# An attention + GELU kernel on one core: planner reserve by unit size, three more GELU chunks on VectorE, and two load times moved

## The chip, the cores and the metric

The kernel runs on one core of a Trainium2 chip. The time is device microseconds for one execution; 5 runs are taken and the median is the number that counts. The engines are named as in the profile: PE (TensorE, matmuls), PEld (its weight loads), DVE (VectorE), ACT (ScalarE), POOL (GpSimd, which here only issues DMAs) and SP (SyncE, which here only issues DMAs).

## The reference

Attention over keys that are pooled 4 x 4, and then a feed-forward layer with a sigmoid-approximated GELU:

```python
# q (4, 12288, 128), kv (4, 384, 32, 128), w_sr (128, 128)
kv_pool = kv.reshape(B, H // r, r, W // r, r, C).mean(axis=(2, 4))   # r = 4: 768 keys per batch
k = v = kv_pool.reshape(B, -1, C) @ w_sr
s = (q @ k.transpose(0, 2, 1)) / sqrt(C)
a = softmax(s)
x = (a @ v).reshape(49152, 128)
h = x @ w_in                                  # w_in (128, 2048)
g = h * (1 / (1 + exp(-1.702 * h)))
out = g @ w_out                               # w_out (2048, 128), out (49152, 128) float32
```

## The kernel before

**Tiles.** The 49152 rows are cut into 96 groups of 512 rows. A chunk is one 128 x 512 tile of intermediate values. An attention group has 6 chunks (768 keys by 128), a feed-forward group has 16 (2048 features by 128). The work goes in two rounds of 48 groups: attention of round 1, feed-forward of round 1, attention of round 2, feed-forward of round 2.

**Units.** ACT takes a unit of up to three chunks in one instruction: PE fills up to three PSUM banks (0 to 2 or 3 to 5, in turn; L347 for attention, L593 for the feed-forward), and one ACTIVATE writes exp (L349) or GELU (L595) of the whole unit to SBUF (tile `ag`). The first two units have 1 chunk, the next 28 have 2, all others have 3, but for the last 8 of the kernel, which have 2 again. PE then drains the chunks: attention chunks in matmuls of 129 columns (L360; a step of `drain_attn` is three matmuls) and feed-forward chunks in matmuls of 512 columns (L603). The last group is drained by `drain_last` (L631), where the last 16 matmuls need the last ACT unit. DVE evicts the sums (L383 and L386 after attention, L614 after the feed-forward).

**VectorE's own share.** DVE computes some chunks without ACT. 24 attention chunks of groups 48 to 51 and 8 "rolling" chunks (the last key chunk of groups 38, 44, 57, 63, ...) go through a polynomial (L428 to L441). The "lent" chunks are feature chunk 15 of some feed-forward groups of round 2: PE fills one bank (L406), `lent_gelu` runs 15 DVE instructions on it (L450 to L472), and the result goes to a buffer `aside` of three slots, from where PE drains it (L603 out of `aside`). `early_fits` says when such a chunk may begin: a lent chunk of group i not before group i - 2 is being filled, a rolling chunk not before its queries are in SBUF. The drain of group i begins only when the lent chunk of i is made.

**Order.** The kernel writes the order of all engines by hand. A planner runs while the program is written: it keeps a model time `now` for PE, `end[p]` for ACT's end of unit p, `dve` for VectorE and `free` for the banks. One model step is one matmul of 512 columns. A unit takes ACT 0.295 + 1.978 steps per chunk; a `drain_attn` step is 0.78, a `drain_moe` step 1.0; half a reciprocal of `lent_gelu` is RECIPROCAL = 10.5. After filling unit n + 2 the planner puts drains and other jobs ahead of the fill of unit n + 3 as long as they end before `limit`:

```python
limit = end[-1] - K - HANDOVER if n + 3 < len(seq) else 1e9     # K = 3, HANDOVER = 1.0
```

`end[-1]` is ACT's end of unit n + 2, the last one filled, and K stands for the fill of unit n + 3. A fill of unit p starts no earlier than `end[p - 2] + HANDOVER / 2`, because it writes the banks that unit p - 2 leaves.

**Loads.** Queries come as bf16 in 24 blocks s of four groups. From block 3 on, POOL's queue casts a block in DRAM (`cast_q`, L209) and SP's queue loads it transposed (`load_qT`, L215, after a one-column DVE memset of the buffer, L214). `background(i)` issues these at the start of attention group i: `TURN` gives the transposing loads, `CAST` the casts. A `gate()` is a DVE memset (L517) followed by a POOL memset (L518), so that POOL's queue stays behind the order of DVE. The load of `w_in` (L548) stands at group 27 and that of `w_out` (L551) at 28. On SP the transposing loads share one queue with `put_away` (L500) and `bring_back` (L506), which transpose the attention output through DRAM.

Of the kernel before, what the change touches and what calls it, by code (L numbers as in the profile page):

```python
# [24 lines left out]
def kernel(  # L25
# [10 lines left out]
    FCH = d_ff // 128  # L36
# [5 lines left out]
    GB = NG // B  # L42
    SB = NS // B
    K = 3
# [53 lines left out]
    def acc_bf():  # L98
        return acc().bitcast(BF)
# [18 lines left out]
    kv_tiles, kv_sums, pooled, pTs, kTs, vs = {}, {}, {}, {}, {}, {}  # L118
# [86 lines left out]
    qTs = {}  # L205

    def cast_q(s):
        sl = slice(s * SG, (s + 1) * SG)
        nc.gpsimd.dma_start(out=q_bf[sl, :].rearrange("(p i) c -> p (i c)", p=128),  # L209
                            in_=q_flat[sl, :].rearrange("(p i) c -> p (i c)", p=128))  # L210

    def load_qT(s):
        qTs[s] = qpool.tile([128, 1, SG], BF, name="qT")
        nc.vector.memset(qTs[s][:, 0, 0:1], 0.0)  # L214
        nc.sync.dma_start_transpose(out=qTs[s], in_=q_bf[s * SG:(s + 1) * SG, :])  # L215


    QS = 3
    qs = [x_tile(XS - 1 - JC - s) for s in range(QS)]

    def load_q(s, lo, hi):
        nc.gpsimd.dma_start(  # L222
            out=qs[s].rearrange("p (g e) -> p g e", g=4)[:, lo:hi, :],
            in_=q_flat[s * SG + lo * G:s * SG + hi * G, :].rearrange("(g p i) c -> p g (i c)", p=128, i=4))

    def transpose_q(g):
        s = g // 4
        if g % 4 == 0:
            qTs[s] = qpool.tile([128, 1, SG], BF, name="qT")
        ps = acc_bf()[:, 0:G].rearrange("p (i t) -> p i t", i=4)  # L230
        for i in range(4):
            o = (g % 4) * G + i * 128
            nc.tensor.transpose(ps[:, i, :], qs[s][:, o:o + 128], ident)  # L233
        dst = qTs[s][:, 0, (g % 4) * G:(g % 4 + 1) * G].rearrange("p (t i) -> p t i", i=4)
        src = ps.rearrange("p i t -> p t i")
        if g == 0:
            nc.scalar.copy(dst, src)
        else:
            nc.vector.tensor_copy(dst, src)
# [86 lines left out]

    early = range(NG // R, NG // R + EARLY)
    rolling = [(i, JC - 1) for i in [*range(38, NG // R, 6), *range(57, 90, 6)]]
    lent = [(g, FCH - 1) for g in range(52, 94, 3)]
    aside = agpool.tile([128, K, 512], BF, name="aside")  # L330

    def weights(c):
# [112 lines left out]
    def lent_gelu(ps, out):  # L445
# [23 lines left out]
        for m in (0, 256):  # L469
            nc.vector.reciprocal(b[:, m:m + 256], a[:, m:m + 256])  # L470
            yield RECIPROCAL
        nc.vector.scalar_tensor_tensor(out, raw, -LN2 / 1.702, b, MUL, MUL)  # L472
# [4 lines left out]
    made, used = {}, []  # L477
# [4 lines left out]
    def early_fits(p, i, jc):  # L482
        if (i, jc) in rolling:
            group = seq[p][1][0][0] if seq[p][0] == "a" else seq[p][1][0][0] // (NG // R) * (NG // R) + NG // R - 1
            return (i // GB, jc) in vs and i // 4 - 1 <= group // 4 and len(used) > rolling.index((i, jc)) - K
        if (i, jc) in lent:
            return seq[p][0] == "m" and seq[p][1][0][0] >= i - 2 and len(used) > len(rolling) + lent.index((i, jc)) - K
        return low and min(slot_of.values()) >= low and (2, JC - 1) in vs
# [24 lines left out]
    def gate():  # L513

        one = gate_tile[:, gates[0] % 8:gates[0] % 8 + 1]
        gates[0] += 1
        nc.vector.memset(one, 0.0)  # L517
        nc.gpsimd.memset(one, 0.0)  # L518

    TURN = {6: 3, 7: 4, 8: 5, 20: 6, 21: 7, 22: 8, 30: 9, 32: 10, 35: 11, 40: 12}  # L520
    CAST = {0: [5], 13: [6], 14: [7], 15: [8], 25: [9, 10], 26: [11, 12]}
    CAST_MOE = {20: 13, 21: 14, 22: 15, 23: 16, 33: 17, 34: 18, 35: 19, 36: 20, 37: 21, 38: 22, 39: 23}

    def background(i):

        first_round = i < GB * 2
        s = TURN.get(i, NS) if first_round else i // 4 + 3 if i % 4 == 0 else NS
        if s < NS:
            load_qT(s)
        if i in CAST:  # L530
            gate()
            for s in CAST[i]:
                cast_q(s)
        if i in (10, 12):
            gate()
            for jc in range(i % 10 * 3 // 2, i % 10 * 3 // 2 + 3):
                load_chunk(1, jc)
        if 0 <= i - 16 < JC:
            extras.append((key_and_value, 1, i - 16))
        if 0 <= i - 15 < JC:  # L540
            extras.append((pool_chunk, 1, i - 15))
        if i in (28, 33, 38):
            put_away(0, (i - 28) // 5)
        if i in (31, 36, 41):
            bring_back(0, (i - 31) // 5)
        if i == 27:
            gate()
            nc.gpsimd.dma_start(out=w_in_sb, in_=moe_w_in)  # L548
        if i == 28:
            gate()  # L550
            nc.gpsimd.dma_start(out=w_out_sb, in_=moe_w_out.rearrange("(o p) c -> p o c", p=128))  # L551

# [99 lines left out]
    seq, todo = [], []  # L652
# [90 lines left out]
    FIXED, CHUNK, SWITCH, HANDOVER, EVACUATE = 0.295, 1.978, 6.0, 1.0, 4.5  # L743
# [2 lines left out]
            transpose_pooled: (0.9, 3.6), make_k: (0.8, 3.2), make_v: (0.8, 3.7)}  # L746
    COPY = {pool_chunk: 1.5, key_chunk: 1.5, value_chunk: 1.5, key_and_value: 2.8, transpose_q: 3.2}
    SMALL = 0.26
    RECIPROCAL = 10.5
    PAUSE = 4.0  # L750
    end, extra_at = [], 0.0
    source, dve = None, 0.0
# [41 lines left out]
    for n in range(len(seq)):  # L794
        fill(n + 2)
        jobs(n + 3)
        while True:
            room = room_ahead()
            limit = end[-1] - K - HANDOVER if n + 3 < len(seq) else 1e9
            bank = free[next_acc()]  # L800
            f = None
            if extras and now >= max(extra_at, bank):
                f, *args = extras[0]
            if steps and dve <= now + 2.0:
                early_step()
            near = todo and todo[0][0] == "m" and todo[0][2] > 10
            if not f and not near and not steps and early_todo and early_fits(min(n + 2, len(seq) - 1), *early_todo[0]) and dve <= now + 2.0 and now >= bank:
                f, args = early_fill, early_todo[0]
            if f and max(now, bank) + COST[f][0] > limit + (0.0 if f is early_fill else 4.5) and room >= 4 * K:
                f = None  # L810
            if f:
                now = max(now, bank) + COST[f][0]
                f(*args)
                free[last_acc] = dve + 1.0 if f is early_fill else copied(f)
                if f in (transpose_pooled, make_k, make_v):
                    on_dve(2.5)
                extra_at = max(now + PAUSE, dve + 1.5 if f in (transpose_pooled, make_k, make_v) else 0.0)
                if f is early_fill:
                    pass
                else:  # L820
                    extras.pop(0)
                continue
            if not source:

                if todo_early and not any(early_waits(t) for t in range(todo_early[0][1], todo_early[0][1] + TS)):
                    source = todo_early
                else:
                    source = todo
            if not source:
                break  # L830
            kind, i, c = source[0]
            needs = at[("at" if kind == "a" else kind, i, c)]
            cost = K * SMALL if kind == "a" else 1.0
            halved = kind == "a" and i // TS < SPLIT
            first_of = (c == 0 or halved) and (kind == "m" or i % TS == 0)
            if source is not todo_early and (needs > n or (kind == "a" and first_of and at["at", i + TS - 1, c if halved else 1] > n)
                                             or (kind == "m" and first_of and (i, FCH - 1) in lent
                                                 and made.get((i, FCH - 1), 1e9) > now + 1.0)
                                             or (kind == "a" and (early_waits(i) or first_of and early_waits(i + TS - 1)))):
                if first_of:  # L840
                    source = None
                break
            start = now if source is todo_early else max(now, end[needs] + HANDOVER)
            if first_of:
                start = max(start, bank)
            if start + cost > limit and not (room < 2 * K + 1 or (room < 4 * K and start == now)):
                if first_of:
                    source = None
                break
            now = start + cost  # L850
            (drain_attn if kind == "a" else drain_moe)(i, c)
            source.pop(0)
            if kind == "a" and i // 4 in early:
                early_left -= 1
                if not early_left:
                    low = 0
            if (halved or c == (1 if kind == "a" else FCH - 1)) and (kind == "m" or i % TS == TS - 1):
                source = None
# [31 lines left out]
```

The softmax here doesn't subtract the row's maximum and nothing guards it: scores larger than these inputs give would overflow.

## Time and profile before

| what | value |
|---|---|
| median of 5 runs | 950.36 us (950.16 to 951.31) |
| the profiled execution's own time | 950.16 us |
| its span in the profile | 948.4 us |
| PE busy | 935.0 us (99%) |
| ACT busy | 934.9 us (99%) |
| DVE busy | 536.3 us (57%) |
| POOL busy | 66.5 us (7%) |
| mean granted TensorE clock | 1.00 |

The page gives busy time by engine, by slices of time and by groups of instructions. The end of a matmul in it is modelled, and some matmul records are missing, so how full PE is must be read from the starts of matmuls and from the count of weight loads (one for each matmul), not from PE's busy share. The time outside of the span is 1.8 us.

### The profile page before, as it was taken

How to read it: one execution, taken by the hardware profiler on the slowest of the kernel's cores; microseconds unless marked ns; L12 is line 12 of the kernel's file. 1: busy time of each engine (PE TensorE's matmuls, PEld its weight loads, DVE VectorE, ACT ScalarE, POOL GpSimd, SP SyncE). 2: the span in 40 equal slices, each digit the busy share in tenths (PEclk: the TensorE clock that was granted, in tenths of full speed). 3: DMA queues.
4: the chain of work that ended last, by engine and by line, in shares of the span. 5: the costliest groups of instructions: out<-in, count | busy, mean ns of one | idle time of the engine just before them, and what ended most of it. 6: DMA issues, size and time to landing. Idle time of an engine off the chain costs nothing.

```text
span 948.4 us, 15310 instructions
## 1 busy us (share of the span) xinstructions
PE 935.0 (99%) x6201; PEld 503.0 (53%) x6314; DVE 536.3 (57%) x1035; ACT 934.9 (99%) x710; POOL 66.5 (7%) x114
## 2 busy tenths in 40 slices
PE   8999999999999999999999999999999999999998
PEld 4677776444444444454446777754444444444444
DVE  5643653102577777778655765365666665566631
ACT  6999999999999999999999999999999999999998
POOL 3101001420000232000000000000000000000000
PEclk9999999999999999999999999999999999999999
DMA  9999932999868799764335683562222222222222
GB/s 210 208 170 198 203 62 45 159 125 174 158 130 120 111 153 117 123 103 79 64 56 116 130 164 74 132 122 36 43 36 44 34 46 34 45 33 45 34 45 45
DMA packets 372855, 95.46 MB, mean 101 GB/s; under 512 B 346720, under 2 KB 370400, under 8 KB 372320
## 3 DMA queue, kind: packets, MB, share of 16 engines
q1 hardware_dynamic: 344000, 62.36, 37.4%
q0 software_dynamic: 28512, 31.99, 22.2%
q8 instruction: 49, 0.80, 0.4%
q14 instruction: 22, 0.18, 0.1%
q10 hardware_dynamic: 272, 0.13, 0.0%
HBM read 52.49 MB, written 48.76 MB: 107 GB/s over the span
## 4 chain that ended last, share of the span: by engine, by line
ACT 88%; PE 9%; DMA 2%; issue 1%; DVE 0%; POOL 0%; POOLq 0%
ACT ag L595 71%; ACT ag L349 17%; PE banks L347 4%; PE banks L360 3%; DMA qT<-q_bf 1%; DMA x<-in_kv_dram 1%; PE banks L139 0%; PE banks L593 0%; PE banks L631 0%; ACT L595 0%; PE banks L233 0%; PE banks L603 0%; ACT L349 0%; DVE kT L163 0%; POOL x L222 0%
## 5 line engine op out<-in xcount | busy, mean ns | idle before, releaser
L595 ACT ACTIVATE ag<-banks 128x1536 bf16<-128x1536 f32 (+1 forms) x510 | 682.2, 1508 | 0.0
L593 PE MATMUL banks<-x,w_in_sb 128*128 128x512 bf16 x1485 | 407.5, 379 | 2.0 <-ACT ag L595 0.3
L603 PE MATMUL banks<-ag,w_out_sb 128*128 128x512 bf16 x1476 | 403.2, 379 | 2.0
L349 ACT ACTIVATE ag<-banks 128x1536 bf16<-128x1536 f32 (+2 forms) x192 | 245.8, 1442 | 3.6 <-PE banks L233 2.3
L603 PEld LDWEIGHTS <-w_out_sb 128*128 128x128 bf16 x1520 | 148.5, 98 | 178.0 <-issue 0.9
L593 PEld LDWEIGHTS <-w_in_sb 128*128 128x128 bf16 x1522 | 147.3, 98 | 170.4 <-issue 1.1
L614 DVE STREAM_TRANSPOSE o_sb<-banks 128x512 f32<-128x512 f32 x95 | 67.9, 715 | 210.9 <-PE banks L603 195.2
L360 PEld LDWEIGHTS <-ag 128*128 128x128 bf16 x2272 | 146.1, 98 | 46.3 <-issue 0.6
L360 PE MATMUL banks<-v,ag 128*128 128x129 bf16 x2272 | 163.7, 220 | 0.2
L347 PE MATMUL banks<-qT,kT 128*128 128x512 bf16 x499 | 145.0, 379 | 3.5 <-DVE kT L163 1.0
L439 DVE SCALAR_TENSOR_TENSOR ea<-ea,eb 128x512 f32<-128x512 f32 x128 | 87.9, 686 | 3.2
L383 DVE RECIPROCAL rec<-banks 128x3 f32<-128x3 f32 x124 | 22.3, 180 | 95.9 <-PE banks L360 95.9
L386 DVE TENSOR_TENSOR x<-banks,rec 128x384 bf16<-128x384 f32 x124 | 69.2, 558 | 4.3
L347 PEld LDWEIGHTS <-kT 128*128 128x128 bf16 x544 | 46.3, 98 | 26.5 <-DVE kT L163 1.7
L470 DVE RECIPROCAL eb<-ea 128x256 f32<-128x256 f32 x28 | 47.6, 1726 | 0.5
L173 POOL DMA_DIRECT2D kvs<-in_kv_dram x32 | 40.5, 1318 | 16.0 <-DMA kvs<-in_kv_dram 12.5
L428 DVE TENSOR_SCALAR ea<-banks 128x512 f32<-128x512 f32 x32 | 22.1, 692 | 32.9 <-PE banks L412 32.6
L463 DVE SCALAR_TENSOR_TENSOR ea<-ea,eb 128x512 f32<-128x512 f32 x56 | 38.3, 684 | 1.6
L518 POOL MEMSET gate_tile<- 1x1 f32 x37 | 3.9, 105 | 328.2 <-DVE gate_tile L517 328.2
L434 DVE SCALAR_TENSOR_TENSOR eb<-eb,ea 128x512 f32<-128x512 f32 x32 | 22.1, 690 | 0.9
L450 DVE TENSOR_SCALAR qT<-banks 128x512 f32<-128x512 f32 x14 | 9.7, 692 | 17.2 <-PE banks L406 16.9
L441 DVE SCALAR_TENSOR_TENSOR ag<-ea,ee 128x512 bf16<-128x512 f32 x24 | 16.5, 688 | 0.7
(83 smaller groups left out, 266.4 us busy)
## 6 DMA issues: line engine op xcount, KB each, us to landing
out_dram<-o_sb SPq DMA_DIRECT2D x380, 64.0 KB, 2.0
kvs<-in_kv_dram POOLq DMA_DIRECT2D x32, 384.0 KB, 6.3
q_bf<-in_q_dram POOLq DMA_DIRECT2D x21, 512.0 KB, 6.8
x_bf<-x SPq DMA_DIRECT2D x13, 768.0 KB, 5.8
x<-in_kv_dram POOLq DMA_DIRECT2D x11, 512.0 KB, 10.1
x_bf<-x SPq DMA_DIRECT2D x6, 384.0 KB, 4.6
x<-in_q_dram POOLq DMA_DIRECT2D x5, 256.0 KB, 15.4
x<-in_kv_dram SPq DMA_DIRECT2D x1, 1024.0 KB, 5.0
```

What stands on the lines that cost most here:

```text
L173: nc.gpsimd.dma_start(out=kv_sums[b][:, i2], in_=kv_p[b, i, w, :, i2], **({"accum_op": ADD} if n else {}))
L347: nc.tensor.matmul(ps[:, k, :], kTs[i // GB][:, jc * 128:(jc + 1) * 128], rhs, start=True, stop=True)
L349: nc.scalar.activation(place([("a",) + c for c in chunks]), ps, AF.Exp, scale=scale)
L360: nc.tensor.matmul(av_of[u][:, k * (C + 1):(k + 1) * (C + 1)], weights(("a", i, jc))[:, o:o + T], vs[i // GB][:, jc, 0:C + 1], start=(jc = ...
L386: nc.vector.tensor_tensor(to, ps[:, :, 0:C], rec.unsqueeze(2).broadcast_to([128, TS, C]), MUL)
L439: nc.vector.scalar_tensor_tensor(a, a, COEFFS[k], b, ADD, MUL)
L463: nc.vector.scalar_tensor_tensor(a, a, COEFFS[k], b, ADD, MUL)
L470: nc.vector.reciprocal(b[:, m:m + 256], a[:, m:m + 256])
L593: nc.tensor.matmul(ps[:, k, :], w_in_sb[:, fc * 128:(fc + 1) * 128], x[:, g % (4 * XS) * G:(g % (4 * XS) + 1) * G], start=True, stop=True)
L595: nc.scalar.activation(place([("m",) + c for c in chunks]), ps, AF.Gelu_apprx_sigmoid)
L603: nc.tensor.matmul(o_of[g], w_out_sb[:, fc, :], weights(("m", g, fc)), start=(fc == 0), stop=(fc == FCH - 1))
L614: nc.vector.transpose(o_sb, o_of.pop(g))
```

## The change

Six edits:

- `limit` keeps free the chunks of the unit that is filled next, `len(seq[n + 3][1])`, instead of 3 always. It differs only ahead of units with fewer than 3 chunks.
- 17 lent chunks instead of 14: groups 52, 54, 57, 59, ... 89, 92 (two and three groups apart in turn) instead of 52, 55, ... 91.
- RECIPROCAL in the planner is 8.2 instead of 10.5.
- The cast of query block 9 goes from group 25 to 16, with a gate of its own; the casts of 10 and 11 stand at 26, that of 12 at 27; the loads of `w_in` and `w_out` go from groups 27 and 28 to 28 and 29.
- The transposing load of block 9 goes from group 30 to 25.
- `early_fits` asks of a rolling chunk that its queries were turned by PE (noted in `turned`), or that their block was loaded, is at most one block ahead of the group being filled, and is none of the first three.

```diff
+    turned = set()
+
     def transpose_q(g):
         s = g // 4
+        turned.add(g)
...
-    lent = [(g, FCH - 1) for g in range(52, 94, 3)]
+    lent = [(g, FCH - 1) for g in range(52, 94) if g % 5 in (2, 4)]
...
-            return (i // GB, jc) in vs and i // 4 - 1 <= group // 4 and len(used) > rolling.index((i, jc)) - K
+            return (i // GB, jc) in vs and (i in turned or i // 4 in qTs and i // 4 - 1 <= group // 4 and i >= 4 * QS) and len(used) > rolling.index((i, jc)) - K
...
-    TURN = {6: 3, 7: 4, 8: 5, 20: 6, 21: 7, 22: 8, 30: 9, 32: 10, 35: 11, 40: 12}
-    CAST = {0: [5], 13: [6], 14: [7], 15: [8], 25: [9, 10], 26: [11, 12]}
+    TURN = {6: 3, 7: 4, 8: 5, 20: 6, 21: 7, 22: 8, 25: 9, 32: 10, 35: 11, 40: 12}
+    CAST = {0: [5], 13: [6], 14: [7], 15: [8], 16: [9], 26: [10, 11], 27: [12]}
...
-        if i == 27:
+        if i == 28:
             gate()
             nc.gpsimd.dma_start(out=w_in_sb, in_=moe_w_in)
-        if i == 28:
+        if i == 29:
             gate()
             nc.gpsimd.dma_start(out=w_out_sb, in_=moe_w_out.rearrange("(o p) c -> p o c", p=128))
...
-    RECIPROCAL = 10.5
+    RECIPROCAL = 8.2
...
-            limit = end[-1] - K - HANDOVER if n + 3 < len(seq) else 1e9
+            limit = end[-1] - len(seq[n + 3][1]) - HANDOVER if n + 3 < len(seq) else 1e9
```

## The prediction

> **What bounds the kernel now.** I read the page's busy shares first, then the windows view of the last stage, then the waits of PE, ACT and SP, and last the timeline around each wait.
>
> ```profile
> PE 935.0 (99%) x6201; PEld 503.0 (53%) x6314; DVE 536.3 (57%) x1035; ACT 934.9 (99%) x710; POOL 66.5 (7%) x114
> ...
> 700.00:800.00 100.00, 99.53 (x456) 45.36 (x464) 64.12 (x89) 100.00 (x75) 0.00 (x0) 1.00 0.25 38
> ```
>
> The second line is 100 us of feed-forward of round 2. ACT runs 75 units in 100.00 us, 1.333 us each, with no gap: it is full. The columns in the brackets count instructions: 464 weight loads, so 464 matmuls, of which 8 have no record. In the timeline three 512-column matmuls start every 0.647 us (917.63, 918.28, 918.92), 0.2157 each. 464 x 0.2157 = 100.1 us: PE is full as well.
>
> Here a rule of the Trainium skill speaks against that reading. "Perfetto Trace Analysis", section "Identifying the Most-Contended Engine", says that matmul busy time is a poor measure and that the busy share of the weight loads should be used. By it PE, at 45 to 53%, has half its time free, ACT alone sets the time, and what ACT is spared comes off the end. By the starts, PE has nothing free, and sparing ACT alone gives nothing beyond the places where PE waits for ACT. I go by the starts. So I look for gains on both engines and take the smaller.
>
> Where does PE still wait? After the start-up there are three places.
>
> ```profile
> 33.13 0.59 PE L347 MATMUL banks<-qT,kT 128*128 128x512 bf16 x2
> 33.56 0.50 PE L360 MATMUL banks<-v,ag 128*128 128x129 bf16 x6
> 34.04 0.59 PE L347 MATMUL banks<-qT,kT 128*128 128x512 bf16 x2
> 34.47 0.50 PE L360 MATMUL banks<-v,ag 128*128 128x129 bf16 x6
> ```
>
> First, the units of two chunks at the beginning. A cycle is 0.915 us (33.13 to 34.04, and so on to 37.71). Its work is 2 x 0.2157 + 6 x 0.0567 = 0.77 us (twelve 129-column matmuls take 0.68: 39.51 to 40.19). PE stands 0.146 us in each cycle, waiting for ACT to give the banks back.
>
> ```profile
> 92.26 4.53 SPq L215 DMA_TRANSPOSE qT<-q_bf  x1
> ...
> 99.91 0.39 PE L412 MATMUL banks<-qT,kT 128*128 128x512 bf16 x1 [0.25 <-DMA qT<-q_bf]
> ...
> 101.16 1.45 ACT L349 ACTIVATE ag<-banks 128x1536 bf16<-128x1536 f32 x1 [0.32 <-PE banks L347]
> ```
>
> Second, the transposing load of block 9, issued at group 30, lands 7.6 us later, when PE already stands at the rolling chunk of group 38 that needs it. From 99.16, six matmuls would end at 99.50; the next starts at 99.91, so PE loses 0.41 us. ACT stands too: by the starts of its units it loses 0.44 us there (0.32 of it seen as idle).
>
> ```profile
> 935.54 0.38 PE L603 MATMUL banks<-ag,w_out_sb 128*128 128x512 bf16 x1
> 936.24 0.59 PE L593 MATMUL banks<-x,w_in_sb 128*128 128x512 bf16 x2 [0.32 <-ACT ag L595]
> 936.67 0.59 PE L603 MATMUL banks<-ag,w_out_sb 128*128 128x512 bf16 x2
> 937.16 0.59 PE L593 MATMUL banks<-x,w_in_sb 128*128 128x512 bf16 x2
> ...
> 941.75 0.59 PE L593 MATMUL banks<-x,w_in_sb 128*128 128x512 bf16 x2
> 942.19 3.07 PE L631 MATMUL banks<-w_out_sb,ag 128*128 128x128 bf16 x52
> ```
>
> Third, the units of two chunks at the end: 0.27 us at 936.24 (one matmul there has no record), four times 0.056 (0.915 - 4 x 0.2157), 0.1 at 940.82: 0.6 us. Yet behind the last fill PE has a queue of 52 matmuls, 3 us, where ACT's last unit ends at 943.5 and only the last 16 matmuls need it; these start at about 944.2. So PE stood still while it had work that it did later, and the end lies 0.6 us behind what ACT would allow.
>
> **The change part by part.**
>
> *Three more lent chunks.* The feed-forward of round 2 has 751 chunks for ACT instead of 754: 245 units of three and 8 of two, where it was 246 and 8. ACT is spared one unit, 1.33 us. PE's matmuls stay the same, only their place changes: 0 for PE. DVE gets 15 instructions per chunk, by the rows of the page and of the groups view: 4 x 0.684 (L463) + 2 x 1.726 (L470) + 4.86 for the other nine = 11.05 us, 33 us for three. "ScalarE: Activation LUTs", "Rules for kernel authors", says of exp and gelu that ScalarE is the only option; by price it is right, as a chunk costs ACT 0.444 us and DVE 25 times that. If DVE were on the path, the edit would cost 33 us. The row that decides is
>
> ```profile
> L614 DVE STREAM_TRANSPOSE o_sb<-banks 128x512 f32<-128x512 f32 x95 | 67.9, 715 | 210.9 <-PE banks L603 195.2
> ```
>
> DVE waits 195 us for PE ahead of this eviction. Cost 0, under that cover; without it see the second rival. An eviction caught behind a DVE step has cost PE 0.107 us (641.69, 852.67), twice in 14 chunks: 0.02 us for three.
>
> *RECIPROCAL 8.2.* Half a reciprocal takes 1.726 us, 8.0 steps of 0.2157. The model now agrees; the DVE steps of a chunk are written 2 x 2.3 x 0.2157 = 1.0 us closer. No cost, and what makes two groups' distance possible.
>
> *The reserve.* Ahead of units of two chunks `limit` moves one step later. In steps from `end[p - 2]`: the fill starts at 0.5 and ends at 2.5; `limit` was 8.5 - 4 = 4.5, so two drains of 0.78 fit (4.06), not three (4.84); the next fill may start at 4.75. That is the standing time: 0.69 steps, 0.149 us by the model, 0.146 in the trace. Now `limit` is 5.5 and a third drain fits. Nine matmuls and a fill are 0.94 us, over the cycle's 0.915, so PE becomes full, and ACT loses nothing while the delay stays below the second unit's reserve. Six such cycles stand from 32.6 to 37.7 (0.89 us), four smaller waits for ACT between 27.6 and 32.2 add about 0.35: 1.2 us. The waits for a fresh kT at 19 to 25 (0.6 of the idle that the waits view gives) may be partly filled too; between 0 and 0.6 I take 0, since the first drains exist only from 18.7. A reordering there could also push a fill back; its bound below zero is another loss of the size that ACT's starts show there already, 0.6. At the end, feed-forward drains cost 1.0 and two used up 4.5 exactly; three fit now. All 0.6 us of standing can be filled from the queue.
>
> *Block 9.* The load moves from the memset at 92.1 to group 25, whose gate is at 77.85. Its cast, behind gate 16 at about 54 (gate 15 is at 51.9), follows the cast of block 8, which lands at 65.1, and lands near 68, casts being 2.5 apart at 89.7 and 92.1. So the load lands near 86 and the 0.41 us on PE and 0.44 on ACT go. The next thing late would be block 11 (lands 112.3, rolling chunk of 44 near 121): not late. *What is moved past:* on SP, `put_away` of group 28, issued at 73.7, now stands behind this load and goes at about 82; its readers `bring_back` lie at 96.8 and later, and the feed-forward starts at 142: 55 us of cover. The casts of 10 and 11 stay in place or come earlier; that of 12 comes 2 us later and is wanted at 120. `w_in` and `w_out` land at 94.6 and 98.3 now, about 2 us later then; wanted at 142. Blocks 6 to 8 share the DMA engines with the new cast: up to 2.5 us later, with 9 us between block 6's landing (69.2) and group 24 (about 78). POOL has nothing behind gate 16 until 77.9. One gate more is 0.06 us of DVE. *early_fits* changes nothing here: for groups 38 and 44 and later the block is in `qTs` whenever the old condition held. All of this 0.
>
> **Sum.** PE: 1.2 + 0.41 + 0.6 = 2.2 us. ACT: 1.33 + 0.44 = 1.77, plus the 0.6 by which the end lies behind ACT: 2.4. The smaller is 2.2. Against the profiled execution, 950.16 - 2.2 = 947.96; the median lies 0.2 above it, so 948.2.
>
> **The rivals.**
>
> *Given back on PE (36%).* The third drain finds nothing ready, or the new order makes other waits (a fill behind an accumulator bank, an eviction behind a DVE step, 0.1 to 0.3 us apiece, as at 54.76, 122.37 and 566.52). Then only the 0.41 of block 9 and part of the 0.6 stay: 0.4 to 1.4 us, 949.0 to 950.0, and ACT idles instead. For it: PE had such waits in every attention stage. Against: at 40 us 58 chunks had been filled and some 28 drained (114 matmuls of L360, four a chunk), so there is work to take. That the change does nothing at all is only possible for `early_fits`.
>
> *VectorE late at two groups' distance (14%), slower.* A lent chunk takes 13.6 us from L450 to the end of L472 (894.5 to 908.1), evictions included; two groups last 13.4 (L614 every 6.69). A second chunk that waits for the first makes the drain of its group wait, and PE stands with nothing to do. The margin now: the last chunk is made at 908.1, the drain of its group starts near 913.3. So it decides when DVE is over 5.2 us behind. Eight pairs are two apart; if each is 0.6 us beyond the margin, PE loses 4.8 us, 953. Against it: the three groups after each pair give 6.7 us back, and the chain shrinks by 1.0.
>
> *ACT alone decides (within the first case).* If the weight-load rule were right, 1.77 to 2.4 us: 948.0 to 948.6. The time hardly tells it from mine; PE's waits do.
>
> **How the numbers follow.** A measurement of this kernel can tell about 0.2%, 1.9 us. My forecast, 50%, lies at 947 to 948.5, the lower end with the kT waits and some of ACT's early losses won too. It is over the bound only just, so much of the 36% lies right beside it. The range 946.8 to 951.2 takes in the forecast, the first rival and a reordering that costs 0.8; outside are the slow rival and a few in a hundred on either side.
>
> **What would show it.** ACT has 509 GELU activations (L595) instead of 510, L470 runs 34 times. Fills near 33 to 37 are 0.94 apart with nine matmuls between some of them. The 0.25 wait of L412 is gone and the load lands near 86. Near the end three drains stand between fills, and fewer than 52 L631 follow the last fill. I am wrong if waits of PE for DVE grow beyond 1 us, if the first stage of ACT loses more than now, or if L603 out of `aside` waits for L472.

## The result, and the profile after

| what | before | after |
|---|---|---|
| median | 950.36 us (45 runs) | 949.27 us (25 runs) |
| ratio, 95% interval | | 0.9987 (0.9982 to 0.9992) |
| the profiled execution's own time | 950.16 us | 949.27 us |
| its span | 948.4 us | 947.2 us |

The change wins 1.1 us, 0.13%. The forecast was 2.2 us: the time lies inside the range (946.8 to 951.2), but so does the time of the kernel before, and the likeliest case, faster by more than 0.2%, did not come about. The span of the profile fell by more than the time: its median is 947.1 us over the executions of the changed kernel and 948.5 to 948.6 for the kernel before (taken beside the later runs). The time outside of the span rose from 1.8 us to 2.1 us, in every execution alike (2.07 to 2.18). What takes it is not in the profile. In the changed kernel the lines of the core loops stand three further down: L596 and L606 are the fill and the drain of the feed-forward, L350 and L363 those of attention, L415 and L409 the single fills for VectorE, L634 the drain of the last group.

First the page of the changed kernel (busy times, the chain that ended last, the reciprocals of the lent chunks), then one row of its windows view:

```profile
PE 934.5 (99%) x6200; PEld 502.8 (53%) x6314; DVE 568.8 (60%) x1081; ACT 934.1 (99%) x709; POOL 66.7 (7%) x115
...
PE 97%; ACT 1%; DMA 1%; issue 1%; DVE 0%; POOL 0%; POOLq 0%
...
L473 DVE RECIPROCAL eb<-ea 128x256 f32<-128x256 f32 x34 | 57.8, 1726 | 0.6
```

```profile
700.00:800.00 100.00, 99.47 (x454) 45.25 (x463) 69.32 (x97) 100.00 (x75) 0.00 (x0) 1.00 0.26 39
```

ACT has one instruction less, VectorE runs its 34 half reciprocals and is 32 us busier, and the chain is now PE from end to end (97%; before, ACT carried 88% of it, and yet sparing ACT alone gives nothing, as `lent_only` shows below). 463 weight loads in 100 us, at 0.2157 us a matmul, are 99.9 us: PE is as full as before.

The wait for block 9 is gone. SP's queue and PE around the rolling chunk of group 38, from the timeline:

```profile
77.95 2.02 SPq L215 DMA_TRANSPOSE qT<-q_bf  x1
80.03 0.57 SPq L503 DMA_DIRECT2D x_bf<-x  x1
85.74 14.49 SPq L509 DMA_TRANSPOSE x<-x_bf  x1
100.39 5.21 SPq L215 DMA_TRANSPOSE qT<-q_bf  x1
```

```profile
98.80 0.81 PE L350 MATMUL banks<-qT,kT 128*128 128x512 bf16 x3
99.49 0.38 PE L415 MATMUL banks<-qT,kT 128*128 128x512 bf16 x1
99.70 0.50 PE L363 MATMUL banks<-v,ag 128*128 128x129 bf16 x6
```

The load starts at 77.95 (it landed at 82.1) and L415 follows its forerunner with only the 0.04 us more than three matmuls take. `put_away` went behind it, from 73.7 to 80.0, as forecast.

The early units of two chunks and the end, in PE's timeline:

```profile
33.57 0.59 PE L350 MATMUL banks<-qT,kT 128*128 128x512 bf16 x2
34.00 0.67 PE L363 MATMUL banks<-v,ag 128*128 128x129 bf16 x9
34.51 0.59 PE L350 MATMUL banks<-qT,kT 128*128 128x512 bf16 x2
34.94 0.33 PE L363 MATMUL banks<-v,ag 128*128 128x129 bf16 x3
35.38 0.59 PE L350 MATMUL banks<-qT,kT 128*128 128x512 bf16 x2
```

```profile
934.76 0.81 PE L606 MATMUL banks<-ag,w_out_sb 128*128 128x512 bf16 x3
935.40 0.59 PE L596 MATMUL banks<-x,w_in_sb 128*128 128x512 bf16 x2
...
940.92 0.59 PE L596 MATMUL banks<-x,w_in_sb 128*128 128x512 bf16 x2
941.36 2.62 PE L634 MATMUL banks<-w_out_sb,ag 128*128 128x128 bf16 x44
```

Nine matmuls stand where six stood, at 0.94 us a cycle (33.57 to 34.51), until a cycle with three gives the delay back. At the end three drains go ahead of a fill (934.76), and 44 matmuls are left behind the last fill, not 52.

**A ledger of PE's waits.** Since PE carries the time, its waits can be added up: in each stretch, the time between the starts of matmuls, less 0.2155 us for one of 512 columns, 0.0563 for one of 128 or 129, 0.026 for one of 32. A matmul without a record is counted by its weight load. PE's work comes to 930.9 us in both kernels. The ledger says where time goes, not why.

| stretch, us | before | after |
|---|---|---|
| 0 to 12, start-up | 4.58 | 4.59 |
| 12 to 40, units of two chunks | 4.51 | 3.74 |
| 40 to 141, attention of round 1 | 1.21 | 0.44 |
| 141 to 604 | 1.69 | 2.56 |
| 604 to 930, feed-forward of round 2 | 0.71 | 0.60 |
| 930 to the end | 0.56 | 0.07 |
| sum | 13.26 | 12.00 |

The sum falls by 1.26 us and the span by 1.2. So PE gained 2.0 us before 141 and at the end, and lost 0.9 between 141 and 604 us, where the change moves no job by intent. Of the 2.0, 1.7 lie in the places that the forecast named (0.77, 0.41 and 0.49). The other 0.4 are two waits ahead of drains, 0.27 at 54.76 and 0.13 at 122.37, which the new order happens not to have.

### The profile page after: what moved, and what is told of

Read it like the earlier page. It is cut to its first block, busy times and chain, and to the rows that moved or that the text cites. A ratio compares the mean times of both kernels' runs of the same rounds, so it can differ in the third digit from the quotient of the medians.

```text
span 947.2 us, 15360 instructions
## 1 busy us (share of the span) xinstructions
PE 934.5 (99%) x6200; PEld 502.8 (53%) x6314; DVE 568.8 (60%) x1081; ACT 934.1 (99%) x709; POOL 66.7 (7%) x115
## 4 chain that ended last, share of the span: by engine, by line
PE 97%; ACT 1%; DMA 1%; issue 1%; DVE 0%; POOL 0%; POOLq 0%
PE banks L606 35%; PE banks L596 34%; PE banks L363 14%; PE banks L350 12%; ACT ag L352 1%; PE banks L415 1%; DMA x<-in_kv_dram 1%; PE banks L139 0%; PE banks L409 0%; PE banks L634 0%; PE banks L236 0%; PE banks L161 0%; POOL x L222 0%; PE banks L294 0%; DVE o_sb L617 0%
## 5 line engine op out<-in xcount | busy, mean ns | idle before, releaser
L596 PE MATMUL banks<-x,w_in_sb 128*128 128x512 bf16 x1487 | 406.7, 379 | 1.2
L606 PE MATMUL banks<-ag,w_out_sb 128*128 128x512 bf16 x1467 | 399.8, 379 | 2.3
L606 PEld LDWEIGHTS <-w_out_sb 128*128 128x128 bf16 x1520 | 148.4, 98 | 177.8 <-issue 0.6
L596 PEld LDWEIGHTS <-w_in_sb 128*128 128x128 bf16 x1519 | 147.0, 98 | 170.6 <-issue 1.0
L363 PEld LDWEIGHTS <-ag 128*128 128x128 bf16 x2272 | 146.1, 98 | 45.4 <-issue 0.2
L363 PE MATMUL banks<-v,ag 128*128 128x129 bf16 x2272 | 164.0, 220 | 0.2
L350 PE MATMUL banks<-qT,kT 128*128 128x512 bf16 x498 | 145.3, 379 | 3.6 <-ACT ag L352 0.5
L442 DVE SCALAR_TENSOR_TENSOR ea<-ea,eb 128x512 f32<-128x512 f32 x128 | 87.7, 685 | 3.2
L350 PEld LDWEIGHTS <-kT 128*128 128x128 bf16 x544 | 46.1, 98 | 25.9 <-issue 1.8
L473 DVE RECIPROCAL eb<-ea 128x256 f32<-128x256 f32 x34 | 57.8, 1726 | 0.6
L466 DVE SCALAR_TENSOR_TENSOR ea<-ea,eb 128x512 f32<-128x512 f32 x68 | 46.6, 685 | 1.9
L453 DVE TENSOR_SCALAR qT<-banks 128x512 f32<-128x512 f32 x17 | 11.8, 692 | 25.7 <-PE banks L409 25.6
```

The costliest lines, as they stand in the source:

```text
L350: nc.tensor.matmul(ps[:, k, :], kTs[i // GB][:, jc * 128:(jc + 1) * 128], rhs, start=True, stop=True)
L363: nc.tensor.matmul(av_of[u][:, k * (C + 1):(k + 1) * (C + 1)], weights(("a", i, jc))[:, o:o + T], vs[i // GB][:, jc, 0:C + 1], start=(jc = ...
L442: nc.vector.scalar_tensor_tensor(a, a, COEFFS[k], b, ADD, MUL)
L466: nc.vector.scalar_tensor_tensor(a, a, COEFFS[k], b, ADD, MUL)
L596: nc.tensor.matmul(ps[:, k, :], w_in_sb[:, fc * 128:(fc + 1) * 128], x[:, g % (4 * XS) * G:(g % (4 * XS) + 1) * G], start=True, stop=True)
L606: nc.tensor.matmul(o_of[g], w_out_sb[:, fc, :], weights(("m", g, fc)), start=(fc == 0), stop=(fc == FCH - 1))
```

## The experiments

Theory A: PE is full, and the time is PE's work and PE's waits; ACT is close behind and takes over when it isn't spared as well. Rival B, after the rule on weight loads: PE has room and ACT sets the time. Times are medians, ratios are to the kernel before on the same chip. That kernel's median was 950.25 us beside `lent_only`, `reserve_only`, `after_old_reserve` and `after_14_lent`, 950.39 beside `after_pe_twice`, the two with the reserve at one end and `after_20_lent`, and 950.35 beside the other four. Span and waits are those of the profiled execution; the last column is the median over all executions.

| kernel | median, us | ratio (95%) | span | sum of PE's waits | outside of the span |
|---|---|---|---|---|---|
| `lent_only` | 950.57 | 1.0001 (0.9994 to 1.0009) | 948.4 | 13.28 | 1.79 |
| `reserve_only` | 951.53 | 1.0013 (1.0006 to 1.0020) | 949.5 | 14.41 | 1.78 |
| `load_only` | 949.83 | 0.9992 (0.9984 to 1.0000) | 948.1 | 12.98 | 1.81 |
| `after_old_reserve` | 950.05 | 0.9993 (0.9986 to 1.0001) | 948.3 | 13.15 | 1.78 |
| `after_14_lent` | 949.89 | 0.9993 (0.9987 to 1.0000) | 948.1 | 12.93 | 1.78 |
| `after_pe_twice` | 951.64 | 1.0011 (1.0004 to 1.0017) | 949.6 | 12.11, and 2.37 more work | 2.16 |
| `after_reserve_end_only` | 949.24 | 0.9985 (0.9979 to 0.9992) | 947.4 | 12.25 | 1.77 |
| `after_reserve_start_only` | 949.61 | 0.9991 (0.9983 to 0.9999) | 947.6 | 12.44 | 2.12 |
| `after_20_lent` | 955.55 | 1.0052 (1.0039 to 1.0065) | 953.5 | 18.42 | 1.78 |
| `after_rec_10` | 949.00 | 0.9984 (0.9978 to 0.9991) | 947.1 | 12.03 | 1.87 |
| `reserve_from_20` | 948.51 | 0.9977 (0.9968 to 0.9985) | 946.5 | 11.40 | 1.85 |
| `reserve_from_24` | 948.73 | 0.9981 (0.9974 to 0.9989) | 946.6 | 11.42 | 1.97 |

In every row the span less the waits is 935.1 to 935.2 us (937.5 with the added work): 930.9 of work, and 4.2 before the first matmul and behind the last. So the waits account for every span. They don't account for the last column, which is as large as some of the differences below (2.14 in the changed kernel) and stays open.

**Is PE full? More work for PE alone.**

```diff
         for k, (g, fc) in enumerate(chunks):
-            nc.tensor.matmul(ps[:, k, :], w_in_sb[:, fc * 128:(fc + 1) * 128],
+            for _ in range(2 if g >= 52 and g % 4 == 0 and fc == 8 else 1):
+                nc.tensor.matmul(ps[:, k, :], w_in_sb[:, fc * 128:(fc + 1) * 128],
...
```

> The changed kernel with 11 fill matmuls of the second feed-forward round done twice over into the same bank (groups 52, 56, ... 92, feature chunk 8): 11 x 0.2157 = 2.37 us more work for PE, none for ACT. Theory A: PE has no room, +2.1 to +2.5 us. Rival B (PE half free, as its weight loads are busy 53%): 0 to +0.3 us.

Measured 951.64, 2.37 us above the changed kernel's 949.27: what 11 matmuls take. Rival B is out: a PE whose weight loads are busy 53% had no more than 0.1 us to spare.

**Sparing ACT alone.** The edit is the two lines of `lent` and RECIPROCAL.

> The kernel before with the 17 lent chunks and RECIPROCAL 8.2 alone. Theory A (PE is full from 40 us on and its waits set the end; ACT is spared for nothing): PE loses no wait but part of the 0.5 us that it stands for ACT in the last units, so 0 to -0.5 us against 950.36. Rival B (ACT sets the time, PE has room): one ACT unit less, -1.3 us.

Measured no change (1.0001; rival B wanted 0.9986, below the interval's lower end at 0.9994). ACT ended earlier, at 942.0 where it had been 943.5, and the span stayed. One unit of ACT, 1.33 us, is worth nothing alone. PE's waits did move, but not for the better. The last stretch of the ledger grew from 0.56 to 0.89 us, since the last group's matmuls now wait for an eviction, 0.47 us by the starts:

```profile
942.04 3.23 PE L631 MATMUL banks<-w_out_sb,ag 128*128 128x128 bf16 x55 [0.30 <-DVE o_sb L614]
```

In the same execution block 9 landed 0.2 us earlier than in that of the kernel before and gave 0.25 us back. That is hardly this edit's doing, as PE's order is the one of before up to 604 us; this load's time from issue to landing was 7.4 to 9.3 us in the traces.

**The reserve alone.** The edit is the line of `limit`.

> The kernel before with the new limit alone. Theory A: PE's early waits shrink by about 1.1 us, but ACT, with 14 lent chunks, is about 0.4 us later out of the early stage and its end then holds PE: 0 to -0.4 us. If PE alone decided, without ACT close behind: -1.5 us. Rival B: ACT's early loss remains, +0.4 us.

Measured +1.2 us: A had it no slower, and B had a third of it. The largest wait is at the rolling chunk of group 38, on PE and on SP's queue:

```profile
98.85 0.81 PE L347 MATMUL banks<-qT,kT 128*128 128x512 bf16 x3
100.96 0.39 PE L412 MATMUL banks<-qT,kT 128*128 128x512 bf16 x1 [1.29 <-DMA qT<-q_bf]
```

```profile
91.61 5.30 SPq L215 DMA_TRANSPOSE qT<-q_bf  x1
```

PE comes to this chunk at 99.50 us, no earlier than in the kernel before. But the block-9 load at its old place, issued 0.65 us earlier than before, took 9.3 us and not 7.6 and lands at 100.9: the wait grows from 0.41 to 1.46 us. Why this load took longer is not shown. The stretch from 141 to 604 us gives back 0.9 us, as in the changed kernel, and the 14 lent chunks leave ACT to end at 945.4, so that the last 16 matmuls wait 0.8 us for it. Against all this stand 0.8 us won between 12 and 40, and the 0.4 us of the two waits at 54.76 and 122.37. With the load moved, the same limit costs nothing: 949.89 in `after_14_lent`, which has both, and 949.83 in `load_only`.

**The moved loads alone.** The edit is `TURN`, `CAST` and the two weight loads.

> The kernel before with the moved casts and loads alone. Theory A: PE's wait of 0.4 us for block 9 goes and nothing else: -0.2 to -0.6 us against 950.36, unless a new wait of PE in the last units takes it. Rival B: -0.44 us by ACT's stall.

Measured -0.5 us (0.9992), PE's wait of 0.41 gone, no other row of the ledger moved by more than 0.24. Theories A and B both expect this; it confirms the size.

The runs also show what nobody had asked. In the three kernels with the load at its old place, the executions of one kernel lie 1.7 to 4.6 us apart (the kernel before 949.86 to 951.58 in 45 and 949.72 to 954.31 in the 59 beside `lent_only`, `reserve_only` 950.25 to 953.97 in 22). In the eleven with the load moved they lie at most 0.7 us apart (`load_only` 949.58 to 950.02 in 13). So the moved loads do not only win 0.4 us of waiting, they take away the long executions. That it is block 9's landing that varies is likely, since it took 7.4, 7.6 and 9.3 us in the three traces, but no trace here shows a long execution of the kernel before.

**The changed kernel with one part taken back.** First the old limit:

> The changed kernel with the old limit (3 chunks always); lent chunks and moved loads stay. Theory A: PE keeps its early waits for ACT and those at the end, and wins the 0.4 us of block 9 alone: -0.4 to -0.9 us against 950.36. Rival B: the unit and the stall of ACT are saved and its early loss is gone as well: -1.8 us, faster than the changed kernel.

Measured 950.05, 0.2 us under the kernel before on the same chip (the interval includes 1), less than the 0.4 to 0.9 of theory A. ACT is earlier by 1.7 us at its end (941.9), yet PE waits for it in each of the last units as before and then 0.47 us for an eviction, as in `lent_only`: 0.89 us in the last stretch. Theory A had left this wait out. Rival B misses by 1.5.

Then the 14 lent chunks of before:

> The changed kernel with the 14 lent chunks of before. Theory A (PE bound, ACT 0.3 us behind it at the end): ACT ends 1.3 us later and takes the end over: 0.8 to 1.1 us slower than the changed kernel, about 950.2. If PE alone decided: no change, 949.3. Rival B: 1.33 us slower, 950.6.

Measured 949.89, 0.6 us above the changed kernel, less than the 0.8 to 1.1 that I expected. By the spans it is 1.0 us (948.1 and 947.1 in the median), and 0.9 by the waits; the time outside of the span is 0.36 us shorter than in the changed kernel. PE has it in one place:

```profile
942.56 0.78 PE L634 MATMUL banks<-w_out_sb,ag 128*128 128x128 bf16 x10
943.97 0.95 PE L634 MATMUL banks<-w_out_sb,ag 128*128 128x128 bf16 x14 [0.63 <-ACT ag L598]
```

The last 16 matmuls wait for ACT's last unit (0.8 us by the starts). So the lent chunks are worth 0 alone and 0.6 in time on top of the rest: they keep ACT out of the way of what PE won.

**The reserve at the start or at the end only.**

```diff
-            limit = end[-1] - len(seq[n + 3][1]) - HANDOVER if n + 3 < len(seq) else 1e9
+            limit = end[-1] - (len(seq[n + 3][1]) if n > 100 else K) - HANDOVER if n + 3 < len(seq) else 1e9
```

and `n < 100` in the second.

> The changed kernel with the new limit at the last units only; the early units keep the old one. Theory A: PE's early waits for ACT come back (0.9 us), ACT's early loss of 0.4 us goes, and the new waits of PE between 160 and 600 us (0.9 us) may change with the order: +0.9 us if these stay, 0 if they go. Rival B: -0.4 us, as ACT is earlier.

> The changed kernel with the new limit at the early units only; the order of PE is the same up to the last units. Theory A: PE stands for ACT again at the end, +0.3 to +0.5 us. Rival B: 0.

With the end only: 949.24, the time of the changed kernel. So the early part of the reserve, 1.2 us of my sum, is worth nothing in time as it was put in. Without it the waits between 12 and 40 are 0.8 us more, those between 40 and 141 0.4 more, and those between 141 and 604 0.9 less (1.68, not 2.56). Of PE's early gain, then, 0.25 us in the ledger and 0.4 in the median spans (947.5 and 947.1) did reach the end of the span, and the longer time outside of it took that away. With the start only: 949.61; the end is worth 0.34 us on top of the start, and 0.81 without it (950.05 to 949.24).

**Where the early gain went.** The changed kernel's units leave the early stage late: ACT's unit 29 starts 0.43 us later than before, and the delay arises in units 13 to 20 (0.06 us at unit 12, 0.44 at unit 20), where pooling, key and turning jobs stand among the drains. PE's timeline of the changed kernel there:

```profile
25.22 1.19 PE L350 MATMUL banks<-qT,kT 128*128 128x512 bf16 x4
26.24 0.39 PE L236 MATMUL banks<-ident,x 128*128 128x128 bf16 x4
26.93 0.59 PE L350 MATMUL banks<-qT,kT 128*128 128x512 bf16 x2 [0.31 <-ACT ag L352]
```

Fills came late and close together (four at 25.22), ACT fell behind, and PE then stood 0.47 us for it. So the new limit was tried for the later part of the early units only, from unit 21 (`n > 17`) and from unit 25 (`n > 21`), with the last units as in the change:

> The changed kernel with the new limit for the early units 21 to 29 and the last ones; units before 21 (where pooling and key jobs are mixed in) keep the old limit. If PE's early gain is lost because ACT is put 0.4 us late there, this keeps 0.6 to 0.9 us of PE's gain and no ACT loss: 948.6 to 948.9. If it is lost to the waits between 160 and 600 us that any such gain of PE brings, because it has then less to drain: 949.2 to 949.4, with those waits still there.

> As the run before, from unit 25 on: 0.4 to 0.7 us of PE's early gain. First case: 948.7 to 949.0. Second: 949.2 to 949.4.

```profile
33.38 0.59 PE L350 MATMUL banks<-qT,kT 128*128 128x512 bf16 x2
33.81 0.67 PE L363 MATMUL banks<-v,ag 128*128 128x129 bf16 x9
34.32 0.59 PE L350 MATMUL banks<-qT,kT 128*128 128x512 bf16 x2
34.75 0.67 PE L363 MATMUL banks<-v,ag 128*128 128x129 bf16 x9
35.26 0.59 PE L350 MATMUL banks<-qT,kT 128*128 128x512 bf16 x2
```

This is PE of the first: full, cycle after cycle. It takes 948.51 us, 1.8 us under the kernel before and 0.8 under the change (0.45 by the median spans; the time outside of the span is back at 1.85). This version beats both: its slowest run, 948.73, lies under the fastest of the changed kernel, 949.11. The second takes 948.73. The ledger of the first:

| stretch, us | after | end only | from unit 21 |
|---|---|---|---|
| 12 to 40 | 3.74 | 4.52 | 3.76 |
| 40 to 141 | 0.44 | 0.82 | 0.82 |
| 141 to 604 | 2.56 | 1.68 | 1.66 |
| 930 to the end | 0.07 | 0.08 | 0.04 |

PE gains the same 0.75 us in the early stage as in the change, ACT's unit 30 is 0.2 late and not 0.4, and the waits in the middle are those of before. In `reserve_from_24` ACT's unit 30 is 0.1 early, and the waits sum up to the same (11.42). The number of the expectation's first case holds (948.51, a little better than its 948.6 to 948.9); its second, that any gain of PE comes back as waits because it has less left to drain, does not.

What stays open is whether ACT's delay is the cause. In the changed kernel PE's new waits in the middle are of two kinds. Those for ACT, at 535.97, 566.86 and 574.92, are 0.42 us in all where they were 0.18 (at 566.52 and 574.58). Those for VectorE's evictions, around the key and value jobs of batches 2 and 3, are 0.7 us: 0.16 at 231.51, 0.16 at 246.36, 0.23 at 246.81 and 0.15 at 406.50. The third of them:

```profile
246.23 0.52 DVE L201 CAST v<-banks 128x384 bf16<-128x384 f32 x1
...
246.81 0.38 PE L415 MATMUL banks<-qT,kT 128*128 128x512 bf16 x1
```

The first kind fits a late ACT, but it is about a quarter of the loss. The second comes with the order of jobs that the planner wrote from its shifted state. Up to 604 us PE's order is one and the same in the kernels with the new limit from the first units on, another in those with the old limit there, and again another in each of the last two. So a late ACT and an unlucky order always came together here; no run changes the one without the other.

**Can VectorE take more?**

```diff
-    lent = [(g, FCH - 1) for g in range(52, 94) if g % 5 in (2, 4)]
+    lent = [(g, FCH - 1) for g in [*range(52, 72, 2), *range(73, 85, 2), *range(86, 94, 2)]]
```

> The changed kernel with 20 lent chunks (two groups apart nearly throughout): ACT has one unit of three less still, 1.33 us. Theory A: nothing to win but the 0.1 us that PE waits for ACT at the end: 0 to -0.2 us. Rival B: -1.3 us. If VectorE cannot follow at two groups' distance, PE waits ahead of drains and it is slower by 1 us or more.

Measured 955.55, 6.3 us above the changed kernel. The timeline at the first of four such places (the others are near 760, 838 and 869):

```profile
726.52 5.53 ACT L598 ACTIVATE ag<-banks 128x1536 bf16<-128x1536 f32 x4
...
728.14 0.81 PE L596 MATMUL banks<-x,w_in_sb 128*128 128x512 bf16 x3
...
728.98 0.65 DVE L475 SCALAR_TENSOR_TENSOR aside<-qT,eb 128x512 bf16<-128x512 f32 x1
...
729.41 0.81 PE L596 MATMUL banks<-x,w_in_sb 128*128 128x512 bf16 x3 [0.46 <-ACT ag L598]
...
730.75 0.81 PE L596 MATMUL banks<-x,w_in_sb 128*128 128x512 bf16 x3 [0.53 <-ACT ag L598]
```

Fill after fill with no drain between them: VectorE finishes a lent chunk only at 729.6 (the end of L475), and in the plan the drain of its group may not begin before. PE stands up to 0.70 us per unit; ten such fills cost 6.3 us. The page names ACT as the releaser, but ACT was at work without a gap; what PE lacked was a drain. At 17 chunks nothing of this is seen (0.60 us of waits from 604 to 930); by the forecast's argument, the three groups after each pair give VectorE its time back.

**The planner's price of a reciprocal.** RECIPROCAL = 10.5 in the changed kernel.

> The changed kernel with RECIPROCAL 10.5 in the planner. The 17 chunks still fit in the plan; the DVE steps lie 1 us further apart. Expected: no change (949.1 to 949.5). If the closer steps are what lets DVE follow at two groups' distance, PE waits ahead of drains: slower by 1 us or more.

Measured 949.00, 0.3 us under the changed kernel, with the same waits (12.03 and 12.00) and the same median span (947.1): all of the 0.3 lies outside of the span. VectorE keeps up without this edit.

## Why the prediction was right, and where it was wrong

The time lies in the stated range, which says little, as the time of the kernel before lies in it too. The account of what bounds the kernel holds; the sum was twice what came.

- *What bounds the kernel*: right. PE is full to within 0.1 us (`after_pe_twice`), ACT stands directly behind it. The rule of the Trainium skill ("Perfetto Trace Analysis", "Identifying the Most-Contended Engine") would have misled here if weight loads alone are taken: they were busy 53% of a PE that was full. The section names MFU (the matmul work done, as a share of the peak) beside them, which the prediction left out.
- *Block 9*, 0.41 us: right. -0.5 us alone (`load_only`); the load landed at 82 (86 expected), and what it was moved past cost nothing. That the move also takes the long executions away was not foreseen.
- *The end*, 0.6 us: right in size. 0.49 in the ledger, 0.34 to 0.81 by experiments.
- *Three lent chunks*, 0 for PE and 1.33 for ACT: right. `lent_only` shows 0, `after_14_lent` shows 0.6 lost when they are missing. The wait for an eviction that they bring at the end when the reserve is the old one (0.47 us) was not foreseen.
- *The reserve at the start*, 1.2 us: this is the step that failed. The third drain went in and PE's standing in the two-chunk cycles fell, but the ledger shows 0.77 us for 12 to 40, and the end-only run shows that 0.25 us of waits and nothing of the time were left at the end. I had said that "ACT loses nothing while the delay stays below the second unit's reserve". That holds in the cycles that I worked out, from 31 us on. The new limit begins at unit 3, and in the mixed units before it put ACT 0.4 us late, which I had bounded at 0.6 and then entered as 0. The 0.9 us of new waits from 141 on came with that delay and with the new order; which of the two makes them is open. `reserve_from_20` shows the size that the step has where its argument applies: 0.7 us (949.24 to 948.51).
- *Luck*: two waits that the prediction had named only as examples of what a new order may bring, at 54.76 and 122.37, went away with the new order, 0.4 us. Without them the change would have won less.
- *The first rival* described what came: a part of PE's gain given back in new waits, at 949.0 to 950.0. It had 36%; the case that I took for likeliest had 50%. The sum took every wait of PE as won and left no term for waits that a new order makes, although the rival named the evictions and the waits for ACT that then appeared.
- *VectorE late*: not at 17 chunks; at 20 it is the mechanism that the second rival described.

## What to carry to other kernels

When two engines are both full, the parts of a change don't add up: sparing ACT alone gave 0, relieving PE alone made it slower, and together with the moved loads they gave 1.1 us. Sum up the starts of the bounding engine against its work before and after, stretch by stretch: the waits account for every span here, and they show which gain is given back where. Compare spans as well as times, as the time outside of the span need not stay the same (1.8 and 2.1 us here). A planner's margin is loosened only for the stretch whose cycle has been worked out; the same line let loose on the units before it left nothing in time of what it had won.

## What the runs showed of the hardware

- A 512-column matmul that was written a second time into the same bank cost its full 0.2155 us: 11 of them, 2.37 us on the median.
- A transposing load is not of one length: at the old place, beside two weight loads and casts on POOL's queue, block 9 took 7.4 to 9.3 us from issue to landing in three kernels (before, `lent_only`, `reserve_only`); at its new place 3.8 to 5.6 in eleven. In the changed kernel the first `bring_back` held SP's queue for 14.5 us (85.74), where it had been 3.7; it was 14.2 to 15.3 in all kernels with the load moved but `reserve_from_24`, where it was 2.9. Nothing needed it for over 30 us; the cause of neither was tried.
